# Attention unit: memory products on 64x64 tiles, phi on ScalarE, fewer weight halves decoded early

## The chip, the cores and the metric

One core of a Trainium2 chip. TensorE (PE; PEld is its weight load) multiplies into PSUM, VectorE (DVE), ScalarE (ACT) and GpSimd (POOL) do the rest, SyncE (SP) issues transfers. The metric is the time of one execution in device microseconds, a median over runs.

## What is computed

Attention with a compressive memory, then two MLP layers. B, H, S, D = 4, 8, 576, 64; 2304 tokens of 512 values; the MLPs are 512 to 2048 to 512. The weights come as 64-bit floats.

```python
def _attn_ref(q, k, v, M_prev, z_prev, beta):
    scores = scale * np.matmul(q, k.transpose(0, 1, 3, 2))      # causal mask, softmax
    ...
    local = np.matmul(a, v)
    def phi(x):
        return np.where(x > 0, x, np.exp(x) - 1.0) + 1.0
    q_p = phi(q)
    mem_ret = np.einsum('bhsd,bhde->bhse', q_p, M_prev)
    mem_norm = np.einsum('bhsd,bhd->bhs', q_p, z_prev)[..., None] + 1e-06
    mem_out = mem_ret / mem_norm
    g = 1.0 / (1.0 + np.exp(-beta))[None, :, None, None]
    return g * mem_out + (1 - g) * local
# then x = h @ w_in; g = piecewise square of h; x = g @ w_out   (_moe_ref)
# then h = x @ w_in; x = max(0.01 h, h) @ w_out                 (_moe2_ref)
```

## The kernel before

The attention runs first, in 16 units, one for each batch row and pair of heads. A unit transposes k and q on TensorE (L483, L484), splits each into a high and a low part (ScalarE copy, VectorE subtraction: L488, L489, L494, L496), multiplies scores in fp32r (`products`, L534 for row blocks 0 to 3, two heads in the two halves of the array; L526 for the last 64 rows), adds the mask and takes the row minimum on VectorE (L553), exponentiates on ScalarE (L558), turns the result (L432; evacuated by ScalarE, L566) and multiplies by v (L588, L584) into the PSUM tile O, 65 columns for a block, the last column being the sum.

Beside that stands the memory branch. phi(q) is made from the transposed q: `exp` from PSUM on ScalarE (f1, L506), the clamp at 1 on GpSimd (f2, L507), `max(q, 0) +` on VectorE (f3, L509); GpSimd copies the last 64 columns apart for the two heads (f4, L516). `memory` (m1, L605, L606) multiplies blocks of 64 rows with a block-diagonal 128x130 of M and z, fp32. VectorE makes the denominators (d1, d2, d3: L611, L622) and the weighted memory part `xm` (L641, L646). The local part `xr` is O times its row factors (totals L627, reciprocal L632, L657, tail L651). GpSimd adds both (x5, L662), TensorE turns the sum back (`back`, L668, L669), ScalarE copies it to `xt` (L672), and SyncE stores it to `x_d`.

During the attention the first MLP's 16 weight halves (128x512 each) are loaded and decoded from 64 bits (`weight_half`: ScalarE L684, VectorE L689, L702, L704, L706, L708, ScalarE L697, GpSimd L693). After the attention, the first MLP works on pairs of 256-token chunks: per pair and 128 hidden rows twelve matmuls of 512 columns (`mm_h`, L788 to L790), ScalarE and VectorE between (L798 to L804), and twelve more (`mm_y`, L818 to L820) two steps later. Jobs such as splitting or decoding weights are put between these steps by number (`at_step`).

The order of the attention on each engine is not written out: `Plan.order` takes tasks with a cost in ns, the tasks they follow, the buffers they need (`Room`) and a priority (unit number times 10 plus a number of the table `PRIO`), and sets one after another. EARLY is the number of halves that the attention decodes; STAY is a price for changing the shape of TensorE's array. PSUM is four rooms W of two banks each.

Of the kernel before, what the change touches and what calls it, by code (L numbers as in the profile page):

```python
# [19 lines left out]
NP = H // 2  # L20
# [19 lines left out]
PRIO = dict(load=-277.95, v=394.34, mem=-13.85, k=43.89, q=50.84, phi=-353.58, f2=-110.59, f3=52.93, f4=327.83, s0=-101.43,  # L40
            s1=-78.43, s2=-165.83, s3=27.93, t0=-222.91, t1=-397.26, t2=60.5, t3=-101.16, v0=60.89, v1=121.75, v2=54.28,
            v3=52.41, m=-55.31, d=162.66, l=-799.7, xm=-237.39, xl=57.15, x=-694.59, b=-388.78, w=(8.6, 23.18, 56.97), c=183.19)
EARLY, STAY = 16, 16.32
# [94 lines left out]
def attn_moe_moe_kernel(ctx, tc, q, k, v, m_prev, z_prev, beta, w1i, w1o, w2i, w2o, out):  # L138
# [33 lines left out]
    for i in range(4):  # L172
        nc.vector.tensor_copy(gates[:, :, 2 * i:2 * i + 2], gate[:, :, 0:2])
        nc.vector.tensor_copy(gates[:, :, 9 + 2 * i:11 + 2 * i], gate[:, :, 2:4])
    for h in range(2):
        r = slice(64 * h, 64 * h + 64)
        nc.vector.tensor_copy(gates[r, :, 8], gate[r, :, h])
        for c in (17, 18):
            nc.vector.tensor_copy(gates[r, :, c], gate[r, :, 2 + h])
# [29 lines left out]
    def new_phi(i):  # L209
        x = att_tile("ph", i, S + 128)  # L210
        nc.gpsimd.memset(x[:, S:S + 128], 0.0)
        return x

    def new_mem(i):
        m = att_tile("mz", i, NP, 132)
        nc.gpsimd.memset(m, 0.0)
        return m, att_tile("zz", i, NP)

# [11 lines left out]
    makers = {"W": lambda i: scratch.tile([128, 1024], F32, name=f"W{i}"), "mem": new_mem, "qs": new_q, "ph": new_phi, "X": new_x,  # L230
# [208 lines left out]
    def attention_unit(u):  # L439
# [6 lines left out]
        ks, qs, ph, st, X, xt = Room("ks"), Room("qs"), Room("ph"), Room("st"), Room("X"), Room("xt")  # L446
# [13 lines left out]
        def spread_z():  # L460
            m, z = at(mem)
            for h in range(2):
                r = slice(64 * h, 64 * h + 64)
                pool.tensor_copy(m[r, :, h], z[r])
# [664 lines left out]
```

## Time and profile before

| | us |
|---|---|
| median of 3 runs | 1041.07 (1040.89 to 1041.52) |
| profiled execution | 1040.5, span 1038.6 |
| busy: TensorE matmul, VectorE, ScalarE, GpSimd | 1003.1, 773.4, 501.3, 130.0 |
| first MLP matmul starts at | 243.30 |

The windows give busy time of each engine in stretches of the span, the groups by line the mean of one instruction, the timeline the place of single ones. Busy time of TensorE runs to a modelled end, so a pace is read from the start of one group to the start of the next. The copy to `xt` that ends a unit starts at 39.68 us for the first unit and at 182.45 us for the eleventh. 195 to 221 us holds two units after the last half is decoded.

### The profile page before, as it was taken

The numbers are of one execution on the slowest core, as the hardware profiler recorded it, in microseconds if no ns is written. First come the engines' busy times: TensorE is split into PE (matmuls) and PEld (weight loads), VectorE is DVE, ScalarE is ACT, GpSimd is POOL, SyncE is SP. The second block draws the span as 40 slices with busy tenths as digits, with TensorE's granted clock in tenths as the row PEclk, the third lists the DMA queues.
The fourth block names the chain that finished last, engine by engine and source line by source line (L and its number), as shares of the span: only waits on it lengthen the run. The fifth ranks groups of instructions, "written<-read, shape, count | busy, mean of one in ns | idle before, by whom it ended". The sixth has DMA issues, their size and how long they took to land.

```text
span 1038.6 us, 20672 instructions
## 1 busy us (share of the span) xinstructions
PE 1003.1 (97%) x8216; PEld 915.3 (88%) x8216; DVE 773.4 (74%) x1764; ACT 501.3 (48%) x829; POOL 130.0 (13%) x167
## 2 busy tenths in 40 slices
PE   7898999998999999999999999999999999999997
PEld 5787778887888888988878889999999999999997
DVE  7999999762436579847757778988878897676656
ACT  5777877673234334633323235544444454343332
POOL 4354534330000000000000000000000001121111
PEclk9999999999999999999999999999999999999999
DMA  9555645311113144303533422232232111113211
GB/s 169 148 142 142 175 120 136 101 35 64 41 41 104 61 150 152 122 22 101 180 124 123 143 86 78 69 135 98 88 101 82 62 41 62 62 68 98 80 41 61
DMA packets 118336, 101.49 MB, mean 98 GB/s; under 512 B 67424, under 2 KB 102496, under 8 KB 118240
## 3 DMA queue, kind: packets, MB, share of 16 engines
q1 hardware_dynamic: 116368, 99.52, 32.2%
q8 instruction: 64, 1.05, 0.4%
q10 hardware_dynamic: 1872, 0.66, 0.3%
q14 instruction: 32, 0.26, 0.1%
HBM read 76.56 MB, written 23.59 MB: 96 GB/s over the span
## 4 chain that ended last, share of the span: by engine, by line
PE 71%; DVE 4%; ACT 1%; issue 0%; POOL 0%; DVEq 0%; ACTq 0%; POOLq 0%
PE A L788 6%; PE A L790 6%; PE A L789 6%; PE A L861 6%; PE A L860 6%; PE A L859 6%; PE y L884 3%; PE y L882 3%; PE y L883 3%; PE y L818 3%; PE y L820 3%; PE y L819 3%; PE A L820 2%; PE A L818 2%; PE A L819 2%; PE h L882 2%
## 5 line engine op out<-in xcount | busy, mean ns | idle before, releaser
L861 PE MATMUL A<-ffn_x,i 128*128 128x256 f32 x576 | 163.1, 283 | 0.0
L859 PE MATMUL A<-ffn_x,i 128*128 128x256 f32 x576 | 163.0, 283 | 0.0
L860 PE MATMUL A<-ffn_x,i 128*128 128x256 f32 x576 | 163.0, 283 | 0.0
L798 ACT ACTIVATE g<-A 128x512 f32<-128x512 f32 (+1 forms) x80 | 44.4, 555 | 241.0 <-PE A L790 241.0
L800 DVE SCALAR_TENSOR_TENSOR g<-A,g 128x512 f32<-128x512 f32 (+1 forms) x80 | 50.9, 636 | 111.9 <-ACT g L799 111.9
L1056 ACT ACTIVATE gh<-g 128x896 fp32r<-128x896 f32 x72 | 68.7, 955 | 124.9 <-PE A L883 72.4
L907 POOL TENSOR_TENSOR ys<-ys,pp 128x512 f32<-128x512 f32 x16 | 27.1, 1715 | 752.3 <-DVE ys L902 752.3
L1035 DVE TENSOR_TENSOR gl<-g,gh 128x896 fp32r<-128x896 f32 x72 | 86.7, 1204 | 33.7 <-ACT gh L1056 33.7
L861 PEld LDWEIGHTS A<-ffn_x,i 128*128 128x128 f32 x576 | 110.6, 192 | 0.0
L859 PEld LDWEIGHTS A<-ffn_x,i 128*128 128x128 f32 x576 | 110.6, 192 | 0.0
L860 PEld LDWEIGHTS A<-ffn_x,i 128*128 128x128 f32 x576 | 110.6, 192 | 0.0
L558 ACT ACTIVATE e<-e,mx 128x512 f32<-128x512 f32 (+2 forms) x144 | 71.6, 573 | 30.9 <-DVE mx L553 30.9
L864 ACT ACTIVATE g<-A 128x512 f32<-128x512 f32 x72 | 42.8, 594 | 88.6 <-PE A L861 88.6
L553 DVE CUSTOM_DVE_ANT_0 e<-W,mask 128x512 f32<-128x512 f32 (+2 forms) x144 | 66.6, 508 | 3.9 <-PE W L534 1.8
L865 DVE TENSOR_TENSOR g<-g 128x128 f32<-128x128 f32 x72 | 29.6, 411 | 46.3 <-ACT g L864 46.3
L788 PE MATMUL A<-ffn_x,i 128*128 128x512 f32 (+1 forms) x160 | 59.7, 373 | 0.0
L789 PE MATMUL A<-ffn_x,i 128*128 128x512 f32 (+1 forms) x160 | 59.3, 371 | 0.0
L790 PE MATMUL A<-ffn_x,i 128*128 128x512 f32 (+1 forms) x160 | 59.3, 371 | 0.0
L789 PE MATMUL A<-xl,i 128*128 128x512 f32 (+1 forms) x160 | 58.9, 368 | 0.0
L788 PE MATMUL A<-xh,i 128*128 128x512 f32 (+1 forms) x160 | 58.9, 368 | 0.0
L790 PE MATMUL A<-xh,i 128*128 128x512 f32 (+1 forms) x160 | 58.8, 368 | 0.0
L566 ACT ACTIVATE pt<-W 128x768 f32<-128x768 f32 (+2 forms) x64 | 51.3, 838 | 8.3 <-PE W L432 8.1
(217 smaller groups left out, 2869.0 us busy)
## 6 DMA issues: line engine op xcount, KB each, us to landing
raw<-in_moe_w_in_dram SPq DMA_DIRECT2D x32, 512.0 KB, 4.0
raw<-in_moe_w_out_dram SPq DMA_DIRECT2D x32, 512.0 KB, 3.3
xf<-y_d SPq DMA_DIRECT2D x18, 512.0 KB, 3.7
xf<-x_d SPq DMA_DIRECT2D x10, 512.0 KB, 4.8
x_d<-xt SPq DMA_DIRECT2D x16, 288.0 KB, 3.9
xf<-yp_d SPq DMA_DIRECT2D x9, 512.0 KB, 4.4
op_d<-ys SPq DMA_DIRECT2D x18, 256.0 KB, 2.3
pp<-op_d SPq DMA_DIRECT2D x9, 512.0 KB, 3.7
```

What stands on the lines that cost most here:

```text
L553: vec.tensor_tensor_reduce(out=out, in0=src, in1=mk, op0=ALU.add, op1=ALU.min, scale=1.0, scalar=3e38, accum_out=at(st)[1][:, col:col + 1])
L558: lambda x=x, w=w, col=col: act.activation(at(x)[:, 0:w], at(x)[:, 0:w], AF.Exp, bias=at(st)[1][:, col:col + 1], scale=-1.0))
L788: nc.tensor.matmul(hx, wh, xh[:, ct], start=(ct == 0), stop=False)
L789: nc.tensor.matmul(hx, wh, xl[:, ct], start=False, stop=False)
L790: nc.tensor.matmul(hx, wl, xh[:, ct], start=False, stop=(ct == 3))
L818: nc.tensor.matmul(o, wh, gh, start=(f == 0 and first), stop=False)
L819: nc.tensor.matmul(o, wh, gl, start=False, stop=False)
L859: nc.tensor.matmul(o, wh, xh[:, ct], start=(s == 0 and ct == 0), stop=False)
L860: nc.tensor.matmul(o, wh, xl[:, ct], start=False, stop=False)
L861: nc.tensor.matmul(o, wl, xh[:, ct], start=False, stop=(s == 1 and ct == 3))
L1035: nc.vector.tensor_tensor(gl, g[:, 1:8], as_r(gh), ALU.subtract)
L1056: nc.scalar.activation(gg[1], gg[0][:, 1:8], AF.Copy)
```

## The change

- `memory` is 20 matmuls of 64x64 weights and 65 columns: each block of 64 rows and each head by itself, h choosing the half of the rows, r the half of the columns. M and z lie without zeros in one tile of 65 columns; phi has no tail copies, and GpSimd's spreading of z goes.
- phi: relu(-q) and exp(-that) on ScalarE, one after the other; GpSimd's clamp goes.
- One denominator instruction for two, one memory multiply of 640 columns for two.
- The tail of the local part adds its memory part on VectorE; GpSimd's sum is 512 columns instead of 640. In the last unit VectorE multiplies and adds in eight instructions, and the transposes follow them in pairs.
- EARLY is 12: four halves (f = 6 and 7) are decoded and split in the first 16 steps of the first MLP.
- `PRIO`, STAY, the costs of decode steps and the assignment of PSUM rooms change, and with them the order everywhere in the attention.

```diff
-EARLY, STAY = 16, 16.32
+EARLY, STAY = 12, 151.79
...
         def load_mem():
-            m, z = at(mem)
+            m = at(mem)
             for h in range(2):
                 r = slice(64 * h, 64 * h + 64)
-                nc.sync.dma_start(out=m[r, :, 2 + 64 * h:66 + 64 * h], in_=m_prev[b, h::2].rearrange("p d e -> d p e"))
-            nc.sync.dma_start(out=z, in_=z_prev[b].rearrange("(p h) d -> (h d) p", h=2))
...
+                nc.sync.dma_start(out=m[r, :, 1:1 + D], in_=m_prev[b, h::2].rearrange("p d e -> d p e"))
+            nc.sync.dma_start(out=m[:, :, 0], in_=z_prev[b].rearrange("(p h) d -> (h d) p", h=2))
...
-            ld_m = add("POOL", 400, "mem", [ld_m], [mem], spread_z)
...
-        f1 = add("ACT", from_psum(S), "phi", [q1], [t, ph], lambda t=t: act.activation(at(ph)[:, 0:S], at(t)[:, 0:S], AF.Exp))
-        f2 = add("POOL", 1600, "f2", [f1], [ph], lambda: pool.tensor_scalar(
-            out=at(ph)[:, 0:S], in0=at(ph)[:, 0:S], scalar1=1.0, scalar2=None, op0=ALU.min))
+        f1 = add("ACT", from_psum(S), "phi", [q1], [t, ph], lambda t=t: act.activation(at(ph), at(t)[:, 0:S], AF.Relu, scale=-1.0))
+        f2 = add("ACT", from_sbuf(S), "f2", [f1], [ph], lambda: act.activation(at(ph), at(ph), AF.Exp, scale=-1.0))
...
-        f4 = add("POOL", 700, "f4", [f3], [ph], phi_apart)
...
         def memory():
-            x, y = at(ph), at(mem)[0][:, p]
-            for r in range(0, 128, 64):
-                for i in range(4):
-                    c, a = 512 + 130 * i if i < 3 else 0, 128 * i + r
-                    pe.matmul(at(m)[r:r + 64, c:c + 130], x[:, a:a + 64], y[:, 0:130], start=True, stop=True)
-                pe.matmul(at(m)[r:r + 64, 130:260], x[:, S + r:S + r + 64], y[:, 2:132], start=True, stop=True)
-
-        m1 = add("PE", 1120, "m", [f3, f4, ld_m], [ph, mem, m], memory, "C")
+            x, y = at(ph), at(mem)[:, p]
+            for i in range(5):
+                for r in range(0, 128, 64):
+                    for h in range(2):
+                        a, c, n = slice(64 * h, 64 * h + 64), 512 * h + W1 * i, 128 * i + r * (i < 4)
+                        pe.matmul(at(m)[r:r + 64, c:c + W1], x[a, n:n + 64], y[a], start=True, stop=True)
+
+        m1 = add("PE", 600, "m", [f3, ld_m], [ph, mem, m], memory, "Q")
...
+        def memory_rows():
+            vec.tensor_tensor(at(X)[1].rearrange("p (i h d) -> p i h d", i=5, d=D), rows_of_m(1, W1),
+                              by_row(sums()[:, 9:19]).unsqueeze(3).broadcast_to([128, 5, 2, D]), ALU.mult)
...
-                vec.tensor_scalar(out=at(X)[0][r, 512 + 64 * h:576 + 64 * h], in0=at(O)[r, 642:642 + D], scalar1=sums()[r, 8:9],
-                                  scalar2=None, op0=ALU.mult)
...
+                vec.scalar_tensor_tensor(out=at(X)[0][r, 512 + 64 * h:576 + 64 * h], in0=at(O)[r, 642:642 + D], scalar=sums()[r, 8:9],
+                                         in1=at(X)[1][r, 512 + 64 * h:576 + 64 * h], op0=ALU.mult, op1=ALU.add)
...
+        def local_last(i):
+            for c in range(2 * i, 2 * i + 2):
+                a = W1 * c if c < 6 else 512 + W1 * (c - 6)
+                vec.scalar_tensor_tensor(out=at(X)[0][:, D * c:D * c + D], in0=at(O)[:, a:a + D], scalar=sums()[:, c:c + 1],
+                                         in1=at(X)[1][:, D * c:D * c + D], op0=ALU.mult, op1=ALU.add)
...
+        if last:
+            x6 = add("PE", 120, "b", [x4], [X, t], lambda: turn_back([4]), "T")
             for i in range(4):
...
+                x5 = add("DVE", 2 * dve(64), "xl", [l2, x1], [X, O, st], lambda i=i: local_last(i))
+                x6 = add("PE", 110, "b", [x5, x6], [X, t], lambda i=i: turn_back([i]), "T")
+        else:
+            x5 = add("POOL", 1300, "x", [x0, x1, x3], [X], lambda: pool.tensor_tensor(
+                at(X)[0][:, 0:512], at(X)[0][:, 0:512], at(X)[1][:, 0:512], ALU.add))
...
     for i, h in enumerate(late):
-        at_step(2 * i + 2, split_half, 0, *h)
-        for _ in range(5):
-            at_step(2 * i, piece, part)
+        at_step(4 * i + 4, split_half, 0, *h)
+        for j in range(5):
+            at_step(4 * i + j // 3 * 2, piece, part)
...
+        order = plan.order()
+        slots_of_w = list(tiles["W"])
+        for slot, i in zip(sorted(range(4), key=plan.rooms["W"].__getitem__), (0, 2, 1, 3)):
+            tiles["W"][slot] = slots_of_w[i]
```

The order on TensorE in a late unit, from its scores (L534) through the last value products to the memory products (L605, L606) and the last score block (L526), before:

```order
L534 MATMUL W_111<-ks_135,qs_123 128x512 x6
L534 MATMUL W_112<-ks_135,qs_123 128x128 x6
L534 MATMUL W_112<-ks_135,qs_123 128x256 x6
L534 MATMUL W_114<-ks_135,qs_123 128x384 x6
L588 MATMUL W_113<-v_147,pt_0_178 64x65 x12
L605 MATMUL W_111<-mz_118,ph_127 64x130 x4
L606 MATMUL W_111<-mz_118,ph_127 64x130
L605 MATMUL W_111<-mz_118,ph_127 64x130 x4
L606 MATMUL W_111<-mz_118,ph_127 64x130
L526 MATMUL W_112<-ks_135,qs_123 128x288 x6
```

The same place now; L507 and L499 are the scores, L561 the values, L579 the memory products, L422 the transposes:

```order
L507 MATMUL W_108<-ks_126,qs_120 128x384 x6
L507 MATMUL W_110<-ks_126,qs_120 128x512 x6
L507 MATMUL W_109<-ks_126,qs_120 128x128 x6
L507 MATMUL W_109<-ks_126,qs_120 128x256 x6
L499 MATMUL W_108<-ks_126,qs_120 128x288 x6
L561 MATMUL W_111<-v_136,pt_0_170 64x65 x16
L579 MATMUL W_108<-mz_113,ph_125 64x65 x20
L422 MATMUL W_109<-ident,e_157 128x128 x3
```

The last score block went ahead of the last values, so the array changes shape two times more in a unit, and the memory products are twice as many with half the columns.

The order on VectorE at the end of the last unit and in the first steps of the MLP, before (L627 and L632 the row factors, L657 and L651 the local part, L800 to L804 the MLP's steps):

```order
L627 SCALAR_TENSOR_TENSOR st_139<-W_112,gates 128x6
L632 RECIPROCAL st_139<-st_139 128x9
L657 TENSOR_TENSOR xr_132<-W_112,st_139 128x384
L657 TENSOR_TENSOR xr_132<-W_112,st_139 128x128
L651 TENSOR_SCALAR xr_132<-W_112,st_139 64x64 x2
L800 SCALAR_TENSOR_TENSOR g<-A,g 128x512
L802 CAST gh<-g 128x512
L804 TENSOR_TENSOR gl<-g,gh 128x512
```

The same place now (L620 the tail, L637 the other multiply-adds, L248 to L257 decoding):

```order
L600 SCALAR_TENSOR_TENSOR st_130<-W_109,gates 128x3
L605 RECIPROCAL st_130<-st_130 128x9
L620 SCALAR_TENSOR_TENSOR xr_117<-W_109,st_130,xm_119 64x64 x2
L637 SCALAR_TENSOR_TENSOR xr_117<-W_109,st_130,xm_119 128x64 x8
L786 SCALAR_TENSOR_TENSOR g<-A,g 128x512
L248 TENSOR_SCALAR da<-raw 128x512
L252 SCALAR_TENSOR_TENSOR da<-w_3499,da 128x512
L788 CAST gh<-g 128x512
L255 TENSOR_SCALAR dr<-da 128x512
L790 TENSOR_TENSOR gl<-g,gh 128x512
```

The sum of the last unit is now VectorE's alone, with the tail ahead, and three decode instructions stand between the first MLP step's own.

The order on GpSimd over one unit before (L507 clamp, L503 tail copies of q, L693 a weight's low part, L516 tail copies of phi, L662 the sum):

```order
L507 TENSOR_SCALAR ph_127<-ph_127 128x576
L503 COPY qs_123<-qs_123 64x2x64 x2
L693 TENSOR_TENSOR o_1475<-w_1173,o_1475 128x512
L516 COPY ph_127<-ph_127 64x64 x2
L662 TENSOR_TENSOR xr_132<-xr_132,xm_134 128x640
```

And over two units now (L485, L679 and L655 in their places):

```order
L485 COPY qs_120<-qs_120 64x2x64 x2
L679 TENSOR_TENSOR i_1074<-w_657,i_1074 128x512
L655 TENSOR_TENSOR xr_117<-xr_117,xm_119 128x512
L485 COPY qs_120<-qs_120 64x2x64 x2
L679 TENSOR_TENSOR o_1282<-w_870,o_1282 128x512
L655 TENSOR_TENSOR xr_114<-xr_114,xm_116 128x512
```

GpSimd keeps three kinds of work of five, with the sum shorter.

## Rows read from the trace of the kernel before

**Rows 1.** Windows: stretch, its length, busy us (instructions) PE PEld DVE ACT POOL, clock, DMA.

```profile
39.68:182.45 142.77, 130.03 (x1824) 114.31 (x1824) 140.14 (x400) 111.45 (x195) 66.26 (x82) 1.00 0.55 140
194.96:221.26 26.30, 26.25 (x384) 23.48 (x383) 17.62 (x67) 19.16 (x35) 8.48 (x12) 1.00 0.20 55
...
243.04:246.44 3.40, 3.40 (x12) 2.72 (x11) 0.00 (x0) 0.65 (x1) 0.00 (x0) 0.50 0.23 87
...
260.00:312.00 52.00, 52.00 (x231) 43.03 (x231) 21.47 (x35) 15.74 (x29) 0.00 (x0) 1.00 0.14 41
```

**Rows 2.** Groups by line, VectorE, weight decode: count, busy us, mean ns of one, idle before.

```profile
L706 DVE SCALAR_TENSOR_TENSOR dr<-raw,dr 128x512 f32<-128x512 uint32 x16 | 16.2, 1015 | 0.3
L708 DVE TENSOR_TENSOR w<-da,dr 128x512 f32<-128x512 f32 x16 | 13.8, 863 | 0.3
L689 DVE TENSOR_SCALAR da<-raw 128x512 int32<-128x512 int32 x16 | 13.8, 862 | 0.2
L702 DVE SCALAR_TENSOR_TENSOR da<-w,da 128x512 int32<-128x512 int32 x16 | 12.5, 779 | 0.6
L704 DVE TENSOR_SCALAR dr<-da 128x512 int32<-128x512 int32 x16 | 9.0, 563 | 0.2
```

**Rows 3.** Timeline, decode instructions beside an idle GpSimd: start us, us, what.

```profile
80.07 0.42 DVE L689 TENSOR_SCALAR da<-raw 128x512 int32<-128x512 int32 x1
...
80.52 0.69 DVE L702 SCALAR_TENSOR_TENSOR da<-w,da 128x512 int32<-128x512 int32 x1
```

**Rows 4.** Timeline, a decode instruction that starts beside GpSimd's sum.

```profile
91.45 1.56 POOL L662 TENSOR_TENSOR xr<-xr,xm 128x640 f32<-128x640 f32 x1 [3.37 <-DVE xr L651]
...
91.55 1.74 DVE L689 TENSOR_SCALAR da<-raw 128x512 int32<-128x512 int32 x1
```

**Rows 5.** Groups by line, GpSimd, attention.

```profile
L507 POOL TENSOR_SCALAR ph<-ph 128x576 f32<-128x576 f32 x16 | 27.3, 1704 | 43.0 <-ACT ph L506 42.9
L662 POOL TENSOR_TENSOR xr<-xr,xm 128x640 f32<-128x640 f32 x16 | 27.2, 1702 | 67.1 <-DVE xr L651 67.1
...
L516 POOL COPY ph<-ph 64x64 f32<-64x64 f32 x32 | 8.5, 267 | 2.6 <-DVE ph L509 0.8 <-DVE st L627 0.4
```

**Rows 6.** Timeline of TensorE from a late unit's last values to its transposes.

```profile
202.35 0.92 PE L588 MATMUL W<-v,pt 128*64 128x65 f32 x24
203.10 1.11 PE L605 MATMUL W<-mz,ph 128*64 128x130 f32 x10
203.99 0.28 PE L606 MATMUL W<-mz,ph 128*64 128x130 f32 x1
204.05 0.27 PE L605 MATMUL W<-mz,ph 128*64 128x130 f32 x1
...
205.03 1.06 PE L526 MATMUL W<-ks,qs 128*128 128x288 f32 x6
205.93 2.34 PE L432 MATMUL W<-ident,e 128*128 128x128 f32 x20
```

**Rows 7.** Groups by line, ScalarE, attention.

```profile
L558 ACT ACTIVATE e<-e,mx 128x576 f32<-128x576 f32 x16 | 12.3, 767 | 0.5 <-DVE mx L553 0.5
...
L684 ACT ACTIVATE w<-raw 128x512 f32<-128x512 f32 x16 | 10.6, 668 | 2.4 <-DMA raw<-in_moe_w_in_dram 2.4
...
L168 ACT ACT_TABLE_LOAD x1 | 1.3, 1283 | 1.8 <-issue 1.8
```

**Rows 8.** Timeline from the last values of the attention to the first MLP matmul.

```profile
238.07 0.87 PE L588 MATMUL W<-v,pt 128*64 128x65 f32 x24
...
239.57 0.75 DVE L657 TENSOR_TENSOR xr<-W,st 128x384 f32<-128x384 f32 x2
240.24 0.57 DVE L651 TENSOR_SCALAR xr<-W,st 64x64 f32<-64x64 f32 x2
240.96 1.53 POOL L662 TENSOR_TENSOR xr<-xr,xm 128x640 f32<-128x640 f32 x1 [7.18 <-DVE xr L651]
...
243.30 0.77 PE L788 MATMUL A<-ffn_x,i 128*128 128x512 f32 x1
```

More of the change, by code (lines that the diff above doesn't have):

```diff
@@ L228, in new_e @@
         return x
[L230 removed]
+    makers = {"W": lambda i: scratch.tile([128, 1024], F32, name=f"W{i}"), "mem": lambda i: att_tile("mz", i, NP, D + 1), "X": new_x,
+              "qs": new_q, "ph": lambda i: att_tile("ph", i, S),
               "ks": lambda i: att_tile("ks", i, 2, S, dt=F32R), "st": lambda i: (att_tile("st", i, 19), att_tile("mx", i, 9)),
@@ L445, in attention_unit @@
         q, k, v = Room("q"), Room("k"), Room("v")
-        ks, qs, ph, st, X, xt = Room("ks"), Room("qs"), Room("ph"), Room("st"), Room("X"), Room("xt")
+        ks, qs, ph, st, X, xt = (Room(x) for x in ("ks", "qs", "ph", "st", "X", "xt"))
         first = "ACT" if u == 0 else "SP"
@@ L656, in local @@
+        x1 = add("DVE", dve(640), "xm", [d3], [X, m, st], memory_rows)
         def local(c, n, at_):
             vec.tensor_tensor(by_head(at(X)[0][:, D * c:D * (c + n)]), heads(at_, n)[:, :, 0:D], weight(c, n), ALU.mult)
-        x0 = add("DVE", dve(384), "xl", [l2], [X, O, st], lambda: local(0, 6, 0))
-        x3 = add("DVE", dve(128), "xl", [l2], [X, O, st], lambda: local(6, 2, 512))
-        x4 = add("DVE", 2 * dve(64), "xl", [l2], [X, O, st], local_tail)
-        x5 = add("POOL", 1600, "x", [x0, x1, x2, x3, x4], [X], lambda: pool.tensor_tensor(at(X)[0], at(X)[0], at(X)[1], ALU.add))
+        last = u == B * NP - 1
@@ new lines, in attention_unit @@
+        if not last:
+            x0 = add("DVE", dve(384), "xl", [l2], [X, O, st], lambda: local(0, 6, 0))
+            x3 = add("DVE", dve(128), "xl", [l2], [X, O, st], lambda: local(6, 2, 512))
+        x4 = add("DVE", 2 * dve(64), "xl", [l2, x1], [X, O, st], local_tail)
+        def local_last(i):
[3 more added lines that the diff above has]
+                                         in1=at(X)[1][:, D * c:D * c + D], op0=ALU.mult, op1=ALU.add)
@@ L663, in attention_unit, with turn_back @@
+        def turn_back(parts=range(5)):
+            x, to = at(X)[0], at(t)
+            for i in parts:
+                if i < 4:
+                    pe.transpose(to[:, 128 * i:128 * i + 128], x[:, 128 * i:128 * i + 128], ident)
+                else:
+                    pe.matmul(to[:, 512:S], x[:, 512:640], pick, start=True, stop=True)
         t = Room("W")
-        def back():
-            x = at(X)[0]
+        if last:
+            x6 = add("PE", 120, "b", [x4], [X, t], lambda: turn_back([4]), "T")
@@ L667, in back @@
             for i in range(4):
-                pe.transpose(at(t)[:, 128 * i:128 * i + 128], x[:, 128 * i:128 * i + 128], ident)
-            pe.matmul(at(t)[:, 512:S], x[:, 512:640], pick, start=True, stop=True)
-        x6 = add("PE", 610, "b", [x5], [X, t], back, "T")
+                x5 = add("DVE", 2 * dve(64), "xl", [l2, x1], [X, O, st], lambda i=i: local_last(i))
+                x6 = add("PE", 110, "b", [x5, x6], [X, t], lambda i=i: turn_back([i]), "T")
+        else:
+            x5 = add("POOL", 1300, "x", [x0, x1, x3], [X], lambda: pool.tensor_tensor(
+                at(X)[0][:, 0:512], at(X)[0][:, 0:512], at(X)[1][:, 0:512], ALU.add))
+            x6 = add("PE", 560, "b", [x4, x5], [X, t], turn_back, "T")
```

79 lines of the change are left out of this document (25 added, 54 removed).

## Prediction

> **What bounds the kernel now.** I read the windows by stage first. From the stored copy of the first attention unit to that of the eleventh (39.68 to 182.45 us, ten units) VectorE is busy 140.14 of 142.77 us, TensorE's matmuls 130.03, ScalarE 111.45 and GpSimd 66.26 [rows 1]. In the window of two late units, where no weights are left to decode, it is the other way round: TensorE 26.25 of 26.30 us, VectorE 17.62 [rows 1]. So a unit costs TensorE 13.15 us (26.30 / 2) and the first ten are held by VectorE at 14.28 us each. From 260 to 312 us, in the first MLP, TensorE is busy 52.00 of 52.00 and VectorE 21.47 [rows 1]. The attention ends at 243.30 us, where the first MLP matmul starts [rows 8], and 795.3 us of the 1038.6 follow; I found nothing in the change that alters those, so the sum is about the time of that first MLP matmul, plus the clock at it.
>
> **VectorE in the ten units.** Decoding a weight half is five VectorE instructions with means 1.015, 0.863, 0.862, 0.779 and 0.563 us: 4.08 us, sixteen times [rows 2]. Inside the ten units the same rows come to 69 of 80 instructions, 13.8 halves, or 57 us of the 140.14; what is left is 83 us, 8.3 per unit. In the changed order I count 49 decode instructions between the same two points, 9.8 halves. The other VectorE edits (one denominator instead of two, one memory multiply of 640 columns instead of 384 and 256) are issue gaps of under 0.1 us a unit; I count nothing for them. So the demand is 83 + 9.8 x 4.08 = 123 us if a half keeps its price.
>
> It should get cheaper. Where GpSimd is idle the instructions take 0.42 and 0.69 us [rows 3]; of the five, two are of the first kind and three of the second, 2.91 us for a half. One that starts beside a GpSimd sum takes 1.74 us and ends when that sum ends [rows 4]. So 1.17 us of the 4.08 is waiting for GpSimd. The change takes from GpSimd the clamp of phi (1.704 us a unit), the tail copies of phi (two of 0.267 us), a fifth of the 1.702 us sum, and four late subtractions [rows 5]: in ten units 66.26 - 17.0 - 5.3 - 3.4 - 4 x 1.3 (four subtractions of 512 columns, estimated at 512/640 of the 1.702, rounded down) = 35 us, from 46% of the time to about 28% of 128. Scaled by that the wait is 0.7 us and a half costs 3.6; VectorE's demand is then **118 us** (bounds: 83 + 9.8 x 2.91 = 111.5, and 123).
>
> **TensorE.** The memory products of one unit stand between 203.10 and 205.03 us: 1.93 us for 20 records (an fp32 matmul leaves two) [rows 6]. They are slow because four 64-column blocks follow one another on the same half of the array: 10 records in 0.89 us, but the turn-over records from one half to the other are 0.06 us apart [rows 6]. Now there are 20 matmuls, 40 records of 65 columns, which go round four 64x64 tiles. No row shows four tiles. Bounds: a record streams 65 columns twice, 54 ns at 2.4 GHz; over four tiles 13.5 ns, 0.54 us in all. The nearest row has two tiles of the same 65 columns: 24 records from 202.35 to 203.10, 31 ns each [rows 6], which gives 1.24 us. The order adds two changes of array shape per unit (scores' last block, then values, then memory, then transposes). One such change is visible: six matmuls of 288 columns need 0.72 us at 2.4 GHz and took 0.90 after the memory products [rows 6], so 0.18 each, 0.36 for two. New price: 0.54 + 0.2 to 1.24 + 0.36; I take the middle of the paces, 22 ns, and 0.36: 1.25 us. **TensorE then needs 12.5 us a unit** (0.65 less; bounds 0.3 and 1.2 less), 125 us for ten units, and becomes the bound there.
>
> The Trainium skill, "TensorEngine Tiling (Array Packing)", Instruction Overhead, speaks against small tiles: each matmul has about 60 cycles of overhead, so a dimension that is already small should not pay for the tiling. By that alone, as an estimate, 40 records would take at least 1.0 us and the gain would be 0.57 us a unit with the two shape changes; no run here shows four tiles yet, and the rows' 31 ns fit it.
>
> **ScalarE.** It gains an exponential of 576 columns from SBUF per unit, 0.767 us, and its share of four halves goes (a copy of 0.668 and one of like shape each) [rows 7]. In ten units 111.45 + 7.7 - 4 x 1.3 = 114 us: 11.4 a unit, no bound by itself, but 91% of the new 12.5. In exchange phi goes relu, exponential, VectorE's sum, instead of a 1.70 us GpSimd step and a tail copy, so the memory products can be ready earlier; what stands behind the added exponential on ScalarE are the key copy and the score exponentials of the next unit, for which TensorE's transposes wait.
>
> **The ten units together.** Demands 125 (TensorE), 118 (VectorE), 114 (ScalarE). Before, the loss over the largest demand was 2.6 us (142.77 - 140.14) with the second engine at 92%. Three engines lie closer now; I allow 4.5 us. 142.8 - 129.7 = **13.1 us** gained. The next three units and the last are TensorE's alone: 4 x 0.65 = **2.6 us**. For the start I count 0 (bounds 2 either way): unit 0's memory products are cheaper, but the first two weight halves are now loaded ahead of M and z.
>
> **The last unit.** Before, VectorE forms the local part from 239.57 (0.75 us for two, 0.57 for the tail), GpSimd adds for 1.53 us from 240.96, and the MLP starts at 243.30: 3.73 us [rows 8]. Now the tail comes first (0.57), then eight 64-column multiply-adds on VectorE, with each transpose right behind its pair. One such instruction lies between 0.1 us (an eighth of the 0.75 for 512 columns) and 0.28 (the tail's, 0.57 / 2, which has the same per-row factor); I take 0.2: 0.57 + 1.6 + 0.4 for the last transposes = 2.6. Gain **1.1 us** (0.5 to 2.0). The granted clock is 0.50 from 243.04 to 246.44 [rows 1], the lower level of 1.2 GHz, after a TensorE that stood still from about 239 to 242.5. That costs 1.7 us. With a product and four transposes strewn into that stretch it may stay up or fall all the same: I count half, **0.8 us**.
>
> **Four halves in the MLP.** Their 4 x 2.91 us of VectorE (GpSimd is idle there) and four splits of about 0.7 lie in the first 16 steps, in which VectorE is idle 59% of the time [rows 1]; the first step has three decode pieces between its multiply-add and its last subtraction, some 1.5 us more, and its result is used only after two more blocks of twelve matmuls. I count nothing; without that cover it would be up to 1.5 us once.
>
> **Sum.** 13.1 + 2.6 + 1.1 + 0.8 = 17.6 us. The profiled execution took 1040.5 us (span 1038.6), the median is 1041.07. 1040.5 - 17.6 = 1022.9; carried to the median, **1023.5 us**.
>
> **Rivals.**
> A, the forecast: TensorE is the bound of the attention. 0.53.
> B, the four tiles really run at once: 0.74 us for memory, TensorE 11.96 a unit. Ten units 119.6 + 4.5, gain 18.7; four units 4.8; the end 2.0 and the clock 1.7: 27 us, 1014 us. For it: two tiles already overlap fully in the 31 ns. Against: weight loads of 64 columns must overlap too. 0.18.
> C, the waits eat it: TensorE keeps the share that it had in the ten units, 131.5 / 142.8 = 92%. Then 125 / 0.92 = 136, gain 7; four units 1.5, the end 0.5: 9 us, 1032 us. For it: three engines with 90% and more, in-order queues, four PSUM rooms, and ScalarE's added exponential ahead of the copies that TensorE waits for. Against: VectorE held 98% beside a TensorE at 92%. 0.20.
> D, slower: the four tiles do not overlap. At 54 ns a record memory costs 2.16 + 0.36 = 2.52 us and TensorE 13.74 a unit; 14 x 13.74 + 5.5 of losses equals what these units take now less the end's gain (142.8 + 40.5 + 13.15 + 1.9 = 198.3): no change, about 1041. That is the point from which it decides; if the 31 ns of a weight load come on top of each record, memory costs 3.76 us, TensorE 14.98, and the time is 1058 us. Against it: the overlap of two tiles. 0.03 for no change and 0.05 for slower.
> E, relu and exponential in turn each load ScalarE's function table: 2 x 1.283 us a unit, ScalarE 14.0 and the ten units near 143 again, 1043 us. Against it: the trace has one load [rows 7] though the MLP's relu follows the attention's exponentials. 0.01.
>
> **Range and chances.** A, B and C hold 0.91 and lie between 1014 and 1032; the bounds of A's unknowns (TensorE 0.3 to 1.2 us a unit, the end 0.5 to 2.0, the clock 0 to 1.7, the start 2 either way) reach 1011 and 1033. About 0.2% is what a measurement of this kernel can tell from none: faster 0.91, same 0.03, slower 0.06.
>
> **What would show it.** In the new profile: the first MLP matmul at about 226.5 us instead of 243.30; two late units 25.0 us apart; the 40 memory records in 0.9 us (0.54 for B, 2.2 or more for D); decode instructions near 3.6 us a half; ten units in about 130 us with TensorE at 96%; the granted clock after the last unit; TensorE still without gaps in the first MLP. I am wrong if the first MLP matmul moves by less than 9 us or the part after it grows.

## The result and the profile after

The changed kernel takes **1009.32 us** (median of 4 runs, 1009.26 to 1010.42) beside 1040.98 for the kernel before: a ratio of 0.9698 (95%: 0.9681 to 0.9715), 31.7 us less. The forecast was 1023.5 and its range ended at 1011: the direction was right, the size was not. The profiled execution took 1010.42 us, its span is 1008.6. The first MLP matmul starts at 213.55 us instead of 243.30, and 795.05 us follow instead of 795.3. The whole gain lies in the attention.

In the changed kernel L507 and L499 are the scores, L561 and L557 the values, L579 the memory products, L422 the transposes, L614 `xm`, L620 the tail, L637 the last unit's eight multiply-adds, L655 GpSimd's sum, L644 and L646 the turning back. Its windows (length, busy us of PE PEld DVE ACT POOL, clock, DMA) answer to [rows 1]: ten units, two late units, the stretch at the half clock, and 52 us of the first MLP.

```profile
36.48:161.50 125.02, 120.30 (x2092) 107.58 (x2093) 117.61 (x360) 113.28 (x199) 33.68 (x41) 1.00 0.62 150
161.50:185.64 24.14, 23.98 (x430) 21.61 (x428) 17.41 (x63) 20.71 (x38) 3.72 (x6) 1.00 0.31 80
212.82:216.24 3.42, 3.39 (x9) 2.44 (x9) 0.55 (x3) 0.65 (x1) 0.00 (x0) 0.50 0.23 90
250.00:302.00 52.00, 52.00 (x231) 43.05 (x230) 26.50 (x45) 18.72 (x34) 0.00 (x0) 1.00 0.24 72
```

The ten units went from 142.77 to 125.02 us. TensorE is now busy 96% of them (120.30 / 125.02) and VectorE 94%, where it was 98% for VectorE. Two late units take 24.14 us, nearly all of it TensorE's. In the MLP VectorE has taken the late halves (26.50 instead of 21.47) and TensorE has no idle time beside it.

The weight decode by line (count, busy us, mean ns, idle before), against [rows 2]:

```profile
L694 DVE TENSOR_TENSOR w<-da,dr 128x512 f32<-128x512 f32 x12 | 9.6, 802 | 0.1
L688 DVE SCALAR_TENSOR_TENSOR da<-w,da 128x512 int32<-128x512 int32 x12 | 9.6, 797 | 0.4
...
L692 DVE SCALAR_TENSOR_TENSOR dr<-raw,dr 128x512 f32<-128x512 uint32 x12 | 8.2, 681 | 0.1
L690 DVE TENSOR_SCALAR dr<-da 128x512 int32<-128x512 int32 x12 | 7.3, 610 | 0.1
L675 DVE TENSOR_SCALAR da<-raw 128x512 int32<-128x512 int32 x12 | 6.4, 536 | 0.1
```

The five means add up to 3.43 us for a half instead of 4.08. TensorE in a late unit, from the end of the scores to the transposes (start, us, line, names, count), against [rows 6]:

```profile
175.81 1.31 PE L507 MATMUL W<-ks,qs 64*128 64x512 f32 x16
177.05 1.06 PE L499 MATMUL W<-ks,qs 128*128 128x288 f32 x6
178.03 1.15 PE L561 MATMUL W<-v,pt 128*64 128x65 f32 x32
179.20 0.81 PE L579 MATMUL W<-mz,ph 64*64 64x65 f32 x40
180.05 2.18 PE L422 MATMUL W<-ident,e 128*128 128x128 f32 x18
```

From the first start to that of the transposes the 40 memory records take 0.85 us, 21 ns each on average, where the 20 longer records took 1.93. The average hides two things. Below are the last 12, 8 and 4 of these records, as seen from three windows (179.87:179.88, 179.93:179.94, 179.985:179.99), each of which shows what had not ended by then:

```profile
179.66 0.35 PE L579 MATMUL W<-mz,ph 64*64 64x65 f32 x12
...
179.72 0.30 PE L579 MATMUL W<-mz,ph 64*64 64x65 f32 x8
...
179.78 0.24 PE L579 MATMUL W<-mz,ph 64*64 64x65 f32 x4
```

Four records start within 0.02 us, and the next four follow 0.058 us after the first ones: 14.6 ns a record. Ten such rounds (five matmuls of two records on each of the four tiles) are 0.58 us; the other 0.26 lies at the ends of the group, most of it between the last record (started at 179.80) and the transposes at 180.05. The end of the last unit, against [rows 8]:

```profile
211.13 0.58 DVE L620 SCALAR_TENSOR_TENSOR xr<-W,st,xm 64x64 f32<-64x64 f32 x2
211.74 1.62 DVE L637 SCALAR_TENSOR_TENSOR xr<-W,st,xm 128x64 f32<-128x64 f32 x8
...
211.86 0.41 PE L646 MATMUL W<-pick,xr 128*128 128x64 f32 x2 [1.37 <-DVE xr L620]
...
212.27 1.62 PE L644 MATMUL W<-ident,xr 128*128 128x128 f32 x4
...
213.55 0.77 PE L774 MATMUL A<-ffn_x,i 128*128 128x512 f32 x1
```

From VectorE's first local part to the first MLP matmul there are 2.42 us instead of 3.73, and the transposes stand inside VectorE's eight steps.

### The profile page after: what moved, and what is told of

Its sections match the earlier page's. It is cut to its first block, busy times and chain, and to the rows that moved or that the text cites. A ratio compares the mean times of both kernels' runs of the same rounds, so it can differ in the third digit from the quotient of the medians.

```text
span 1008.6 us, 21212 instructions
## 1 busy us (share of the span) xinstructions
PE 984.5 (98%) x8536; PEld 899.9 (89%) x8536; DVE 758.7 (75%) x1739; ACT 509.8 (51%) x845; POOL 77.9 (8%) x94
## 4 chain that ended last, share of the span: by engine, by line
PE 73%; DVE 4%; ACT 1%; issue 0%; DVEq 0%; ACTq 0%
PE A L775 6%; PE A L774 6%; PE A L776 6%; PE A L847 6%; PE A L846 6%; PE A L845 6%; PE y L870 3%; PE y L868 3%; PE y L869 3%; PE y L804 3%; PE y L805 3%; PE y L806 3%; PE A L805 2%; PE A L804 2%; PE A L806 2%; PE h L868 2%
## 5 line engine op out<-in xcount | busy, mean ns | idle before, releaser
L531 ACT ACTIVATE e<-e,mx 128x384 f32<-128x384 f32 (+4 forms) x144 | 71.8, 576 | 15.9 <-DVE mx L526 15.8
L526 DVE CUSTOM_DVE_ANT_0 e<-W,mask 128x384 f32<-128x384 f32 (+4 forms) x144 | 66.0, 512 | 2.7 <-PE W L507 2.3
L422 PE MATMUL W<-ident,e 128*128 128x128 f32 x400 | 51.0, 276 | 2.0 <-ACT e L531 0.6
```

Of the source, the lines that this page charges most:

```text
L422: pe.transpose(t[:, c:c + 128], x, ident)
L526: vec.tensor_tensor_reduce(out=out, in0=src, in1=mk, op0=ALU.add, op1=ALU.min, scale=1.0, scalar=3e38, accum_out=at(st)[1][:, col:col + 1])
L531: lambda x=x, w=w, col=col: act.activation(at(x)[:, 0:w], at(x)[:, 0:w], AF.Exp, bias=at(st)[1][:, col:col + 1], scale=-1.0))
```

## The experiments

The question is which of four things carry the 31.7 us: the price of the memory products on TensorE (called T in the expectations), VectorE's relief (phi away from GpSimd, fewer halves), the new order of the queues (O), and the last unit's end. All kernels below compute the whole reference. "Gain" is the difference of the medians to the kernel before on the same chip; ratio and 95% interval are to that kernel too.

**The memory loop.** Two kernels differ from the changed one only in the nesting of the memory loop; every other instruction keeps its place. In `e1_serial` five blocks in a row use the same 64x64 tile; in `e2_two_tiles` the column halves take turns, and the head changes once.

```diff
-            for i in range(5):
-                for r in range(0, 128, 64):
-                    for h in range(2):
+            for r in range(0, 128, 64):      # e1_serial
+                for h in range(2):
+                    for i in range(5):
...
+            for h in range(2):               # e2_two_tiles
+                for i in range(5):
+                    for r in range(0, 128, 64):
```

> The changed kernel with the memory products in another loop order (column half, head, then block), so that five matmuls in a row use the same 64x64 tile; nothing else differs, on any engine. Theory T (TensorE is now the bound of the whole attention, so every microsecond of its work counts): a record costs 54 ns, a unit's products 2.2 us instead of 0.85, TensorE 13.4 us a unit, and the time grows by 16 x 1.3 = 18 to 21 us, to 1028 to 1030. Rival O (the new order and the relief of VectorE made the gain, and TensorE has room): at most 8 us, 1017.

> The changed kernel with the memory products in the loop order head, block, column half: only two tiles take turns, the two column halves. Theory T: 27 to 31 ns a record as the value products have, 1.1 to 1.25 us a unit instead of 0.85, so 16 x 0.25 to 0.4 = 4 to 6.5 us more, 1013 to 1016. Rival O: 0 to 2 us more.

Measured: e1 1022.17 us (ratio 0.9826, 0.9812 to 0.9841), a gain of 18.4; e2 1012.59 (0.9727, 0.9711 to 0.9743), a gain of 28.0. Windows of e1 over its ten units and two late units, and its TensorE around the memory products:

```profile
38.78:170.24 131.46, 129.91 (x2092) 119.64 (x2094) 118.38 (x360) 113.80 (x200) 32.31 (x41) 1.00 0.58 143
183.39:209.71 26.32, 26.29 (x444) 24.09 (x440) 17.60 (x63) 20.71 (x38) 3.71 (x6) 1.00 0.17 47
```

```profile
189.00 2.01 PE L579 MATMUL W<-mz,ph 64*64 64x65 f32 x40
190.94 2.95 PE L422 MATMUL W<-ident,e 128*128 128x128 f32 x25
```

The memory records take 1.94 us (48 ns each), and two late units 26.32 us, as many as in the kernel before (26.30). In e2 they take 1.14 us (29 ns each), and two late units 24.72:

```profile
181.23 1.21 PE L579 MATMUL W<-mz,ph 64*64 64x65 f32 x40
182.37 2.95 PE L422 MATMUL W<-ident,e 128*128 128x128 f32 x25
```

A tile takes its next record 0.058 us after its last one in all three kernels; what the loop order sets is whether one, two or four tiles do so at a time. (In e1 the mean is 48 ns because tiles overlap where one run of five ends and the next begins.) So the same 20 instructions cost 0.85, 1.14 or 1.94 us by their order alone, and four tiles in turn are worth 13 us of the 31.7. T is right in kind but does not carry everything: with TensorE's old price of a unit, 18.4 us stay. Its 1028 to 1030 was too high for two reasons: a record took 48 ns and not 54, and of the 10.9 us that e1 adds to TensorE's work in the ten units only 6.4 show, because the changed kernel has waits there that e1 no longer has. In the ten units of e1 TensorE is the bound without loss: 131.46 us are ten times 13.15. In the kernel before, with that same price, they took 142.77.

**Phi back on GpSimd**, with the planner still setting the order as if both steps were ScalarE's:

```diff
-        f1 = add("ACT", from_psum(S), "phi", ..., lambda t=t: act.activation(at(ph), at(t)[:, 0:S], AF.Relu, scale=-1.0))
-        f2 = add("ACT", from_sbuf(S), "f2", ..., lambda: act.activation(at(ph), at(ph), AF.Exp, scale=-1.0))
+        f1 = add("ACT", from_psum(S), "phi", ..., lambda t=t: act.activation(at(ph), at(t)[:, 0:S], AF.Exp))
+        f2 = add("ACT", from_sbuf(S), "f2", ..., lambda: pool.tensor_scalar(
+            out=at(ph), in0=at(ph), scalar1=1.0, scalar2=None, op0=ALU.min))
```

> The changed kernel with phi as before: exp from PSUM on ScalarE, clamp at 1 on GpSimd; the order on every engine is kept (the clamp stands in GpSimd's queue where ScalarE's exponential stood). Theory T: a decoded half costs VectorE about 4.1 us again instead of 3.4, its demand in ten units goes from 118 to 124 us and passes TensorE's 121, so 3 to 5 us more, 1012 to 1014. Rival S (ScalarE's added exponential holds TensorE up, so taking it away gains): 1 to 4 us less, 1005 to 1008. If neither matters: 1009.

Measured: 1016.36 us (0.9766, 0.9751 to 0.9780), 7 us more than the changed kernel. The ten units and two late units:

```profile
36.38:165.46 129.08, 120.52 (x2072) 107.35 (x2074) 120.87 (x359) 108.23 (x190) 49.65 (x51) 1.00 0.59 145
177.91:202.81 24.90, 24.17 (x443) 21.89 (x441) 17.41 (x62) 19.56 (x36) 6.88 (x9) 1.00 0.20 55
```

VectorE's work grows by 3.3 us (a half costs 3.73), but the ten units by 4.1, and even the late units, which hold no decode, are 0.38 us longer each: TensorE now waits there for phi itself.

```profile
180.18 2.18 PE L508 MATMUL W<-ks,qs 64*128 64x384 f32 x24 [0.29 <-DVE ph L491]
```

VectorE's step of phi (L491) waits for the 1.7 us clamp, the scores for VectorE. Within the new order the move to ScalarE is worth 7 us, more than expected; whatever ScalarE's extra exponential costs (ACT 108 to 113 us) is already taken off. A clamp with an order planned for it may cost less; that was not run.

**Number of halves and the last sum.** `e3_early15` sets EARLY to 15; `e11_early10` sets it to 10, with six halves three steps apart in the MLP; `e5_last_sum_gpsimd` treats the last unit like the others.

```diff
-EARLY, STAY = 12, 151.79
+EARLY, STAY = 15, 151.79             # e3_early15
...
-        last = u == B * NP - 1
+        last = False                         # e5_last_sum_gpsimd
...
+EARLY, STAY = 10, 151.79             # e11_early10
...
-        at_step(4 * i + 4, split_half, 0, *h)
+        at_step(3 * i + 4, split_half, 0, *h)
...
-            at_step(4 * i + j // 3 * 2, piece, part)
+            at_step(3 * i + j // 3 * 2, piece, part)
```

> The changed kernel with fifteen halves decoded in the attention instead of twelve; the planner sets the order anew. Theory T: three halves bring 3 x 3.4 = 10 us of VectorE into the ten units, 128 us against TensorE's 121, so VectorE holds them again at about 130 instead of 125 us: 1014 to 1016. If the decode were covered (TensorE alone sets the pace): 1009 to 1010. Above 1018 the new order itself would be worse.

> The changed kernel with ten halves decoded in the attention and six in the first MLP, three steps apart. After the run with fifteen (1.2 us more) I expect little: TensorE holds the units at 12.06 us and two halves less relieve units that are nearly at that: 1008 to 1009.3. If VectorE still held the ten units: 2 x 3.4 = 6 us less, 1003. If the first MLP no longer hides the decode: above 1010.

> The changed kernel with the last unit's sum by GpSimd as in the other units. The step from the row factors to the first MLP matmul took 3.73 us before and takes 2.42 now: 1.2 to 1.4 us more by the prediction's reading, 1010.5 to 1011. If the sum is hidden: 1009.3.

Measured: e3 1010.79 (0.9707, 0.9692 to 0.9721), some 1.2 us more than the changed kernel and not 5; e5 1011.44 (0.9708, 0.9691 to 0.9724), 1.0 us more by the ratio and 2.1 by the median; e11 1015.62 (0.9760, 0.9747 to 0.9774), 6 more. In e3 the ten units are as long as before the edit, although 11 of the 15 added decode instructions stand in them:

```profile
36.74:161.81 125.07, 119.56 (x2066) 106.88 (x2066) 123.36 (x370) 115.37 (x203) 34.92 (x42) 1.00 0.61 150
```

VectorE does 5.7 us more in the same time: at the changed kernel's 94% it was not the bound, and even at 99% it costs the ten units nothing. The three units behind them, with the other four instructions, take 0.9 us longer (37.11 instead of 36.19). In e5 the step from the first local part to the first MLP matmul takes 3.41 us, 0.99 more than in the changed kernel:

```profile
210.91 0.76 DVE L626 TENSOR_TENSOR xr<-W,st 128x384 f32<-128x384 f32 x2
...
214.32 0.77 PE L774 MATMUL A<-ffn_x,i 128*128 128x512 f32 x1
```

The part from there on is 1.2 us longer, with the clock granted at 0.50 for 6.83 us and not for 3.42. In e11 the attention ends as early as ever (213.23), and the first MLP pays: two gaps in which `mm_y` waits for VectorE's decoded output weights, and 3.4 us at half clock from 266.4 (and none at its start).

```profile
256.98 0.50 PE L806 MATMUL y<-gh,o 128*128 128x512 f32 x1 [2.22 <-DVE o L344]
...
264.94 0.50 PE L806 MATMUL y<-gh,o 128*128 128x512 f32 x1 [2.22 <-DVE o L344]
```

**Parts on the kernel before.** `e8_before_early12` decodes 12 halves, the others in the MLP as in the change. `e9_before_alternating` lets the column halves of the 64x130 products take turns. `e12_before_phi` puts relu and exponential on ScalarE where exponential and clamp stood. `e14_before_three` has all three. All keep the whole old table.

```diff
-EARLY, STAY = 16, 16.32
+EARLY, STAY = 12, 16.32                  # e8, e14
...
-            for r in range(0, 128, 64):
-                for i in range(4):
+            for i in range(5):               # e9, e14
+                for r in range(0, 128, 64):
...
-        f1 = add("ACT", from_psum(S), "phi", ..., AF.Exp))
-        f2 = add("POOL", 1600, "f2", [f1], [ph], lambda: pool.tensor_scalar(
-            out=at(ph)[:, 0:S], in0=at(ph)[:, 0:S], scalar1=1.0, scalar2=None, op0=ALU.min))
+        f1 = add("ACT", from_psum(S), "phi", ..., AF.Relu, scale=-1.0))   # e12, e14
+        f2 = add("POOL", 1600, "f2", [f1], [ph], lambda: act.activation(..., AF.Exp, scale=-1.0))
```

> The kernel before with twelve halves decoded in the attention and four in the first MLP, and nothing else. VectorE's demand in the ten units falls from 140 to 140 - 4 x 4.1 = 124 us, TensorE's 131.5 (13.15 a unit) becomes the bound: ten units in 133 to 136 us, 7 to 10 us gained, 1031 to 1034. If only the new table lets the gain through: under 3 us, 1038 to 1041.

> The kernel before with its ten memory matmuls in another loop order, so that the two 64-column halves of the array take turns; the order on every engine is kept. The products should cost 1.1 instead of 1.93 us a unit. If VectorE holds the ten units, that gains only in the last four units and the start: 2.5 to 5 us, 1036 to 1038. If TensorE held all of the attention: 12 us, 1028.

> The kernel before with phi as in the change (relu, then exponential, both on ScalarE; the exponential stands where GpSimd's clamp stood, all else in the order of before; the tail copies stay on GpSimd). Theory: VectorE holds the ten units and waits for GpSimd; without the clamp's 1.7 us a unit a half costs 3.6 instead of 4.08 us, 13.8 halves 6 to 7 us less, 1033 to 1035. If GpSimd's load does not matter to VectorE, or ScalarE's work takes its place: 1040 or more.

Measured: e8 1037.20 (0.9959, 0.9944 to 0.9974), e9 1038.85 (0.9975, 0.9965 to 0.9984), e12 1041.30 (1.0002, 0.9993 to 1.0011): 4.1, 2.5 and 0 us. In e8 the units are decoded in the same order as before and the first seven keep their length; only those behind come down to 13.1 to 13.4, near TensorE's price. Its ten units take 140.58 us, with TensorE busy for 129.92 of them and VectorE for 126.71. In e9 the 20 records take 1.21 us instead of 1.93, and the ten units show that VectorE does not care:

```profile
39.82:181.52 141.70, 125.49 (x1824) 106.90 (x1824) 139.81 (x400) 111.09 (x194) 66.60 (x82) 1.00 0.56 141
```

TensorE's work falls by 4.5 us there (130.03 to 125.49), the time by 1.1. In e12 GpSimd falls from 66 to 50 us and a half from 4.08 to 3.84, less than expected. Its late units take 13.35 us instead of 13.15, in which TensorE waits 0.2 to 0.3 us for VectorE's step of phi, now behind a second activation; and in its profile 6.83 us of the ten units ran at a granted clock of 0.50, which may hide part of what they gained.

**Order and parts.** The obvious test, the new code with the whole old table, has no order that the planner can find, and the old code with the new table was not run. Three kernels come near. `e6_old_table` is the new code with the old priorities (but the new ones of t0 to t3 and v0 to v3) and STAY 16.32. `e14_before_three`, above, has the parts under the old order. `e16_old_parts` has the new order and the old parts: memory loop of e1, clamp of e4, 15 halves, GpSimd's last sum.

```diff
+PRIO = dict(load=-277.95, v=394.34, mem=-13.85, k=43.89, q=50.84, phi=-353.58, f2=-110.59, f3=52.93, ...   # e6
+EARLY, STAY = 12, 16.32
```

> The changed kernel with the priorities and the shape price of before, save for the eight of the transposes t0 to t3 and values v0 to v3, which stay new (the wholly old table cannot be planned). Theory T: the instructions are the same, so TensorE's work per unit is within 0.4 us and the time within +0 to +7 us, 1009 to 1016. Rival O: most of the 31 us come from the new table and go with it, 1025 to 1040.

> The kernel before, with its whole table of priorities, and three instruction parts of the change together: 12 halves, memory columns halves taking turns (20 records of 130 columns, no 64x64 tiles), relu and exponential on ScalarE in the clamp's place. Alone they gained 4.1, 2.5 and 0 us. Theory Sum (they only add): 1033.5 to 1036. Theory Together (VectorE and TensorE were equal bounds, so that parts which relieve one alone show little and both at once show more; the ten units fall to TensorE's demand of about 127 plus 4.5, the late units to 12.7): 1021 to 1026. Theory Order (without a new table the queues wait for each other, as with the old priorities on the new code): 1033 or more, and in the ten units neither TensorE nor VectorE is busy over 94%.

> The changed kernel's order with the old parts put back: memory products of one tile in a row, clamp on GpSimd, GpSimd's sum in the last unit, 15 halves in the attention. Alone these cost 12.9, 7.0, about 1.5 and about 1.5 us. Theory Sum: 1009.3 + 22.9 = 1032, and about 9 us of the gain are the order's (with the merged instructions). Theory Overlap (with TensorE at the old 13.15 us a unit, VectorE's extra work hides beside it): 1023 to 1027, and the order and the merged instructions carry 14 to 18 us. Theory None (the order carries nothing): 1039 to 1042.

Measured: e6 1040.33 (1.0002, 0.9991 to 1.0013), e14 1035.47 (0.9951, 0.9934 to 0.9967), e16 1039.66 (0.9981, 0.9972 to 0.9991): gains of 0, 5.8 and 1.6 us. The ten units of e6 (6.83 us of them at a granted clock of 0.50):

```profile
40.83:184.63 143.80, 122.53 (x1993) 104.91 (x1994) 118.83 (x354) 110.69 (x191) 31.32 (x38) 0.98 0.50 127
```

of e14:

```profile
39.96:177.61 137.65, 124.25 (x1826) 106.78 (x1827) 124.37 (x381) 111.51 (x195) 45.77 (x69) 1.00 0.53 134
```

and of e16:

```profile
38.96:182.76 143.80, 132.00 (x2073) 118.98 (x2075) 134.00 (x370) 111.37 (x193) 50.08 (x52) 1.00 0.53 130
```

In e14 the work is nearly as light as after the change (124 us on both engines), but each is busy for only 90% of the time: the old order loses 13 us over the larger demand, the new one 4.7 (125.02 less 120.30). In e16 the new order meets 134 us of VectorE and 132 of TensorE and loses 10; each unit takes 14.4 us. The waits of e16's TensorE and VectorE between 60 and 160 us (line <- releaser: us, times, longest) name the place:

```profile
PE W L508 <- DVE ks L471: 4.6, 6, 0.9
PE W L508 <- DVE ph L491: 1.8, 4, 0.6
PE W L500 <- DVE mx L527: 1.4, 2, 0.9
...
DVE ph L491 <- POOL ph L489: 3.7, 6, 0.8
DVE st L591 <- PE W L580: 1.7, 4, 0.8
```

Scores wait for VectorE's half of the key split and its step of phi; VectorE waits for GpSimd's clamp and for the memory products. e6 has the changed kernel's instructions and none of its gain: TensorE has 122.53 us of work in ten units of 143.80. So the table is needed, though e6's is a mixture and no measure of the old one. In sum, the lighter parts alone give about 6 us, the order alone about 2, and 24 of the 31.7 appear only when both are there. e14 lacks the 64x64 tiles, the merged instructions and the last unit's sum, e16 has the merged instructions: the split is one between bundles, not between single edits. Some 5 of the 24 may belong to what e14 lacks: in the new order four tiles instead of two are worth 3.7 us (28.0 to 31.7), the last sum 1 to 2. And neither order was planned for what it met: in e14 the planner still takes phi's second step for GpSimd's, in e16 for ScalarE's. What a fitting order would give either of them is not tested.

**Looking for more.** `e10_keep_busy` fills TensorE's gaps in the last unit's end with 23 transposes of the identity (`busy(n)` makes n of them), whose results are overwritten, to hold the clock. `e13_chunk_gpsimd` gives GpSimd the low part of the MLP's first chunks.

```diff
+            x6 = add("PE", 1200, "b", vs, [t], lambda: busy(11), "T")                 # e10_keep_busy
...
+                x6 = add("PE", 330, "b", [x6], [t], lambda i=i: [pe.transpose(...) for _ in range(3)], "T")
...
-        plan.add("DVE", dve(1024), prio, [t], [raw], lambda: vec.tensor_tensor(       # e13_chunk_gpsimd
+        plan.add("DVE", dve(1024), prio, [t], [raw], lambda: pool.tensor_tensor(
```

> The changed kernel with extra transposes of the identity in TensorE's gaps after the last unit's values (eleven ahead of the tail's product, three ahead of each of the four last transposes); they write PSUM that the real ones overwrite. If the lower clock for 3.4 us at the start of the first MLP comes from these gaps, it is gone and 1.7 us are gained: 1007.6. If the extra work delays the real transposes or the clock falls all the same: 1009.3 or a little more.

> The changed kernel with the low part of the first two token chunks (two subtractions of 1024 columns, 1.2 and 1.9 us of VectorE in the attention) on GpSimd, everything else in the same order. If TensorE's last 4.4 us of waiting in the ten units come from VectorE, 1 to 2 us are gained: 1007.3 to 1008.3. If not: 1009.3; if GpSimd's sum holds VectorE's two-operand work up: above that.

Measured: e10 1009.41 (0.9699, 0.9686 to 0.9712), e13 1009.90 (0.9702, 0.9689 to 0.9715): no gain. In e13 VectorE has less to do, and the ten units take 125.73 us, 0.7 more. The profile of e10 has the clock at 1.00 and the MLP at its full pace at once, three matmuls in 0.78 us, where the changed kernel's first one takes 0.57 until the next:

```profile
213.68 0.48 PE L780 MATMUL A<-ffn_x,i 128*128 128x512 f32 x1
...
214.46 0.39 PE L780 MATMUL A<-ffn_x,i 128*128 128x512 f32 x1
```

Its span is 1007.5 us against 1008.6, yet the medians are equal: the three other executions of the changed kernel span 1007.5 to 1007.6 us as well, at the same mean clock of 0.998 as the profiled one. Where in them the clock was lower is not known. The profiles of e1, e6 and e13 show no fall of the clock there either, without any filling. Nothing tried beats the changed kernel.

## Why the prediction was wrong in size

The forecast missed the median by 14.2 us: 12.5 by the profiled executions, and 1.7 because the profiled execution of the changed kernel is 1.1 us above its median and that of the kernel before 0.6 below. It put the first MLP matmul 16.8 us earlier; it came 29.75 us earlier, 12.95 more. By stretches: the ten units gained 17.75 instead of 13.1, the next three 4.3 instead of 2.0 (40.51 to 36.19), the end 4.5 instead of 1.75 (20.34 to 15.86), the start 3.2 instead of 0 (39.68 to 36.48). The copies that bound these stretches moved against TensorE's work: the ten units hold 980 value records now and 924 before, the start 146 and 176, the end 156 and 200, at some 0.03 us each. Over the whole attention, without such boundaries, the memory products cost 16 x 1.08 = 17.3 us less, TensorE is idle for 15.1 us instead of 26.4, and 1.1 us are left over. The forecast had 9.1 (14 x 0.65) for the first and 7.7 for the second.

**The step that failed: the price of the memory products on TensorE.** The prediction took 1.25 us: 22 ns a record, the middle between four tiles that run at once (13.5) and the two tiles of [rows 6] (31), and 0.36 for two added changes of the array's shape. They took 0.85. The middle was no pace that the array has: the tiles run at once, 14.6 ns a record, which makes 0.30 us of the 0.40, and the ends of the group cost 0.26 and not 0.36. That the average over rounds and ends, 21 ns, is near the 22 is chance.

The rest of the unit cost nothing more. A late unit without its memory products takes 13.15 - 1.93 = 11.22 us before, 12.06 - 0.85 = 11.21 after, 13.16 - 1.94 = 11.22 in e1 and 12.36 - 1.14 = 11.22 in e2. That is a balance and does not show that changes of shape are free: in a unit the transposes behind the memory products grow by 0.30 us (0.25 of it one pause in their middle), and q's and k's transposes, scores and values together shrink by as much. I had priced one visible change of shape and multiplied it, without pricing the whole sequence that the new order prints. I had also misread that one: of the six score matmuls behind the memory products the first takes 0.24 us until the next and the others 0.13, not 0.12, so 0.11 of my 0.18 belongs to the change; 0.09 more stand ahead of it, where the last memory record takes 0.20 until the next instead of 0.11.

A unit fell by 1.09 us, not 0.65; over ten, three and one units that is 6.2 us of the 12.95.

The Trainium skill, "TensorEngine Tiling (Array Packing)", Instruction Overhead, gives about 60 cycles of overhead for each matmul. That would put 40 records at 1.0 us, as an estimate; they took 0.85, and inside the rounds 14.6 ns each, so here it was no floor, and the measurement decides.

**The ten units otherwise came out as reasoned.** VectorE 117.61 us (118 forecast), GpSimd 33.68 (35), ScalarE 113.28 (114), a half 3.43 (3.6). The loss over TensorE's demand is 125.02 - 10 x 12.06 = 4.4 us, where 4.5 were allowed. With 12.06 in the place of 12.5 the ten units would have been right to 0.1. (125 and 4.5 are 129.5, not the 129.7 of the prediction, so its sum is 0.2 too small. And the decode instruction of [rows 4] ends 0.28 us behind GpSimd's sum, not with it.) That the 4.5 was right is more luck than reasoning: e14 and e16 lose 10 to 13 us, e6 21 with the changed kernel's own instructions. The number came from the old loss, but the loss depends on the order, and that I could not price. Rival C (waits eat it, with 92% of the time busy) is what much the same parts do under the old table in e14, with 90%.

**The start was counted at nothing.** It gained 3.2 us. In e1 the first unit ends at 38.78, so 2.3 of these are the overlap of tiles, for the memory products of the first two units that stand in this stretch; the other 0.9 is the moved boundary, 30 value records fewer ahead of the first copy.

**The next three units** were taken for TensorE's alone. The first of them was not: 182.45 to 196.66 is 14.21 us, 1.06 above TensorE's price, with a wait of 1.2 us for VectorE's `xm`, and that went too. I had read the two undisturbed units behind it and applied them to all three.

**The last unit** gained 1.31 at its sum (3.73 to 2.42), near the 1.1; e5's trace puts 0.99 on it. L637's eight instructions take 0.2 us each from start to start, as estimated. The remaining 2.1 us beyond the unit's 1.09 lie ahead of it. The kernel before has a wait of 0.65 us for VectorE's row minimum there:

```profile
229.37 1.16 PE L605 MATMUL W<-mz,ph 128*64 128x130 f32 x10 [0.65 <-DVE mx L553]
```

Some 1.3 us are the moved boundary: TensorE has 44 value records fewer left behind the copy that ends the fourteenth unit. The last 0.1 stays open.

**The clock** was to give back 0.8 us: in the profile it gave none (3.42 us at 0.50, as in [rows 1]). The 1.7 us were also too much for it: the part from the first MLP matmul on takes 793.8 us in the four profiles in which the clock stays up there (e1, e6, e10, e13) and 795.1 to 795.3 in those of before, after, e2 and e3, which is 1.2 to 1.5 us. **The MLP** was right at nothing: 795.05 against 795.3; e11 shows how near the edge that was, since two halves more cost 6 us.

**The rivals.** D and E fall: the tiles overlap, and there is one table load. B holds in its mechanism, and I had given it 0.18: the four tiles run at once, at 14.6 ns a record where it had 13.5, and its unit of 11.96 was reached to 0.1. Its 1014 is still 4.7 us too high. It counts more for the end and the clock than they gave, and nothing for the start (3.2) and for the waits in the eleventh unit (1.06) and ahead of the last sum (0.65). A's own claim, that TensorE becomes the bound of the attention, holds as well. The range's lower end took B's unit, with 2.0 for the end, 1.7 for the clock and 2 for the start; it was passed for the same reasons.

## What to carry to other kernels

Where two engines are within 8% of each other, test parts in bundles: here single edits gave 4, 2.5 and 0 us, an order alone 2, and all together 31.7. Where a row is missing between two mechanisms, do not take the middle of their prices: one of the two holds, and each is a forecast with its own chance. Price a new instruction order by pricing the whole sequence on the bounding engine, not its added penalties alone; what an engine does outside the edited instructions may pay them back. And let small matmuls take turns on different tiles: the loop nest alone moved this kernel by 13 us.

## What the runs showed of the hardware

- 40 fp32 records of 65 columns on 64x64 tiles take 48 ns each with five blocks in a row on one tile, 29 with two column halves in turn, 21 with four tiles in turn. One tile starts its next record 58 ns after its last; four tiles in turn start four records in that time. With 64x130 products, taking turns cuts 20 records from 1.93 to 1.21 us.
- The price of a decoded half does not follow GpSimd's share alone: 4.08 us at 46% (before), 3.73 at 38% (e4), 3.43 at 27% (after), but 4.19 at 35% (e16).
- Behind the same idle gaps at the end of the attention the granted clock fell to 0.50 for 3.42 us in one profile and stayed at 1.00 in that of e13; the fall cost 1.2 to 1.5 us.
